# Four x buffers, a q transpose queued behind an x transpose, and a re-ordered first six microseconds

## The chip, the cores and the metric

One core of a Trainium2 chip. The metric is device time in microseconds (us) of one launch; the number compared is the median of several runs.

## What is computed

Linear attention with a feature map of exponentials, then a two-layer network with a squared ReLU. Cut to its core:

```python
# q, k, v: 8 batches x 8 heads x 576 tokens x 64; w_phi: 64 x 128
def phi(x):
    proj = einsum('bhsd,df->bhsf', x, w_phi)
    proj = proj - max(abs(proj), axis=-1, keepdims=True)
    return concatenate([exp(proj), exp(-proj)], axis=-1)
q_p, k_p = phi(q), phi(k)
kv = einsum('bhsf,bhsd->bhfd', k_p, v)
z = sum(k_p, axis=2)
x = einsum('bhsf,bhfd->bhsd', q_p, kv) / (einsum('bhsf,bhf->bhs', q_p, z)[..., None] + 1e-06)
# x becomes 4608 tokens x 512 (heads side by side); w_in: 512 x 2048, w_out: 2048 x 512
h = maximum(x @ w_in, 0)
out = (h * h) @ w_out
```

## The kernel before

**Work.** The eight batches run one after another through the attention, and 512 tokens of each batch form a chunk of the network; the last 64 tokens of all batches form a ninth chunk. The attention of batch b+1 is interleaved with the first layer of chunk b and the second layer of chunk b-1. TensorE does every product, ScalarE the exponentials, VectorE the maxima, the scaling and the squares; ReLU and copies out of PSUM are shared by the two. PSUM has eight banks, and every group of products is given a bank by a fixed list (`BASES`).

**Order.** The program is first laid down as a list of 1680 numbered operations (`Plan.add`); `ORDER` is a permutation of those numbers, and each engine executes its own operations in that order and never overtakes. An operation waits for its inputs, for its bank and for its buffer. `FILL` puts dummy products of a zero tile (`warm`, line 961) on TensorE ahead of the operations that it names, as (bank, count).

**The start.** Two pieces of k for batch 0 come by ScalarE's queue in float32 and are cast (operations 7 on VectorE, 8 on ScalarE); everything else of q, k, v and the weights comes by GpSimd's queue (13, 14, 12, 19, 9, 10, ... in this order). GpSimd also makes the identity matrix (operation 11, line 913) out of a tile that VectorE has zeroed (operation 5, line 238). With it TensorE transposes the first four blocks of k (40, line 320), VectorE copies them out (41), TensorE projects them (42, line 379), VectorE takes the maxima (48, line 386).

**From attention to the network.** For each block c of a batch (five blocks: four of 128 tokens, one of 64) the products with kv are made in two halves: NA (line 648, feature half one), a scaling of the bank by VectorE (SA, line 660), NB (line 648 again, added into the same bank), then a reciprocal (rd, line 670) and the division into `xo` (line 674), which also sets the bank free. NA of block c=1 and c=2 of batch 0 are operations 148 and 162, with 149/163 for SA and 150/164 for NB. In batch 0 TensorE transposes `xo`; in later batches a DMA transpose does (Xx, line 708, issued by SyncE, called SP here) and writes `xT`, which the first layer reads. `xo` is a ring of three buffers that all batches share, so block number n of the whole program uses buffer n mod 3.

**The first layer of chunk 0** starts block by block, as groups of 16 products of 128 columns (lines 813 and 799) for each quarter of `win`: 303/304 for quarter 0, 307/308 for quarter 1, 311/312 for quarter 2, 315/316 for quarter 3. Their ReLUs are 305, 309, 313, 317.

**SP's queue in the first half** holds, in this order: 373 (transpose of k of batch 2, writes `kT`), 374 (transpose of q of batch 2, writes `qT`), then 266, 275, 284, 293 (the four Xx of batch 1), 564 (transpose of k of batch 3), 302 (Xx of batch 1's short block), and stores. Operations of batch 1 that matter: 265, 274, 283, 292 write `xo` for the blocks c=0 to 3 (292 is block 8, and 266 reads block 5, the same buffer of three); 297 is NA of the short block, in the bank pair that 292 sets free. Operation 422 is the first product that reads batch 2's `qT` (line 347); 482 is the first product of chunk 1's first layer (line 788), and it needs all four Xx.

Of the kernel before, what the change touches and what calls it, by code (L numbers as in the profile page):

```python
# [7 lines left out]
F32 = mybir.dt.float32  # L8
# [100 lines left out]
def kernel(  # L109
# [61 lines left out]
    NQP = 3  # L171
    NQF = 2
# [3 lines left out]
    xo = ring("xo", 3, [8 * D])  # L176
    rden = ring("rden", 3, [8], F32)
# [130 lines left out]
    def attention(b):  # L308
# [279 lines left out]
        def out_halves():  # L588

            slot = qfeat[0]  # L590
            xs = xslot[0] % 3
# [42 lines left out]
        def out_ops(c):  # L634
# [30 lines left out]
            xs = xslot[0] % 3  # L665
# [407 lines left out]
}  # L1073
FILL = {
    40: (0, 26), 42: (0, 11), 74: (0, 5), 76: (0, 7), 58: (0, 10), 60: (4, 10), 92: (0, 7), 131: (0, 16),
    156: (7, 2), 101: (7, 2), 128: (7, 9), 134: (5, 4), 142: (5, 6),
}
TURNED = range(3, 8)
# [29 lines left out]
```

## Time and profile before

| | us |
|---|---|
| runs | 345.08, 345.47, 345.0 |
| median | 345.08 |
| span of the profiled execution, first to last instruction (the profile gives no other time for it) | 344.8 |
| TensorE busy in it | 335.5 |
| VectorE / ScalarE / GpSimd busy | 264.2 / 225.4 / 95.5 |

TensorE is busy for 97% of the span, so the way to read this profile is to look for the few places where TensorE does nothing and ask who ended each of them; time saved on another engine counts only if it ends one of those places sooner. TensorE's dummy products are counted as busy, too.

### The profile page before, as it was taken

Reading aid. Unit: us, or ns where it says so; the run is one execution under the profiler, and the core shown is the slowest. Engines: PE = TensorE matmul, PEld = TensorE weight load, DVE = VectorE, ACT = ScalarE, POOL = GpSimd, SP = SyncE. Lnnn points to the kernel's source line nnn. Section 1 sums busy time; section 2 is a strip of 40 time slices with the busy share of each in tenths; the row PEclk is TensorE's granted clock in tenths of the full one; section 3 lists DMA queues with packets and bytes.
Section 4 is the critical chain, followed back from the end, with each engine's and each line's share of the span. In section 5 each row is a group of like instructions: output and inputs, shape, how many; then the busy total and the mean of one; then the engine's idle time right before and its main releaser. Section 6 shows DMA issues by size and latency. Waiting matters only on the chain.

```text
span 344.8 us, 8417 instructions
## 1 busy us (share of the span) xinstructions
PE 335.5 (97%) x3389; PEld 188.3 (55%) x3389; DVE 264.2 (77%) x485; ACT 225.4 (65%) x393; POOL 95.5 (28%) x143
## 2 busy tenths in 40 slices
PE   8999999799999999999999999999999999999995
PEld 7679776444654555545545554565555444444443
DVE  4999999699877987788898999687876635757510
ACT  4999996489898898476887797798475503210031
POOL 8670671681730390104604051240000000000000
PEclk9999999999999999999999999999999999999999
DMA  9999999999999999999999999999864821101024
GB/s 139 179 206 202 199 132 157 153 118 205 170 175 172 227 165 185 195 182 183 171 207 172 199 164 195 188 154 168 196 125 96 157 62 38 63 0 61 32 68 115
DMA packets 142935, 51.51 MB, mean 149 GB/s; under 512 B 111472, under 2 KB 138416, under 8 KB 142896
## 3 DMA queue, kind: packets, MB, share of 16 engines
q1 hardware_dynamic: 97488, 32.35, 50.7%
q0 software_dynamic: 44960, 18.23, 46.7%
q8 instruction: 26, 0.43, 0.5%
q10 hardware_dynamic: 448, 0.39, 0.4%
q14 instruction: 13, 0.11, 0.1%
HBM read 36.73 MB, written 9.44 MB: 134 GB/s over the span
## 4 chain that ended last, share of the span: by engine, by line
PE 87%; DMA 6%; DVE 3%; ACT 1%; POOL 1%; issue 0%; POOLq 0%; DVEq 0%; SPq 0%
PE psum L788 32%; PE psum L882 31%; PE psum L648 5%; PE psum L462 5%; PE psum L347 5%; DMA xT<-xo 4%; DMA qpn<-qf 3%; PE psum L827 2%; PE psum L569 1%; DVE mk L405 1%; PE psum L813 1%; PE psum L799 1%; PE psum L846 1%; PE psum L450 1%; PE psum L320 1%; PE psum L961 1%
## 5 line engine op out<-in xcount | busy, mean ns | idle before, releaser
L882 PE MATMUL psum<-wout,h 128*128 128x512 bf16 x560 | 132.6, 380 | 0.0
L788 PE MATMUL psum<-xT,win 128*128 128x512 bf16 x448 | 106.1, 379 | 0.6 <-DMA xT<-xo 0.6
L765 ACT ACTIVATE hr<-psum 128x512 bf16<-128x512 f32 x98 | 57.1, 600 | 57.7 <-PE psum L788 50.2
L882 PEld LDWEIGHTS <-h 128*128 128x128 bf16 x560 | 51.1, 98 | 56.5 <-issue 0.3
L788 PEld LDWEIGHTS <-win 128*128 128x128 bf16 x512 | 46.7, 97 | 51.9 <-DMA xT<-xo 1.4
L774 DVE TENSOR_TENSOR h<-hr 128x512 bf16<-128x512 bf16 x144 | 56.0, 415 | 18.7 <-ACT hr L765 18.2
L544 ACT ACTIVATE qf<-psum 128x1024 bf16<-128x1024 f32 (+1 forms) x50 | 46.1, 939 | 5.5 <-PE psum L347 2.0
L405 DVE TENSOR_REDUCE mk<-psum 128x8 f32<-128x1024 f32 (+1 forms) x38 | 42.4, 1120 | 3.9 <-PE psum L347 2.0
L411 ACT ACTIVATE kn<-psum 128x1024 bf16<-128x1024 f32 (+1 forms) x38 | 35.7, 948 | 8.2 <-PE psum L347 4.7
L411 ACT ACTIVATE kp<-psum 128x1024 bf16<-128x1024 f32 (+1 forms) x38 | 35.8, 951 | 4.8 <-PE psum L347 4.0
L648 PEld LDWEIGHTS <-qpn 128*128 128x128 bf16 x624 | 27.5, 97 | 16.6 <-issue 3.1
L767 DVE TENSOR_SCALAR hr<-psum 128x512 bf16<-128x512 f32 x46 | 31.1, 684 | 5.7 <-PE psum L788 4.2
L660 DVE TENSOR_TENSOR psum<-psum,en 128x520 f32<-128x520 f32 (+1 forms) x39 | 27.2, 702 | 10.3 <-PE psum L648 6.1
L648 PE MATMUL psum<-kv,qpn 128*128 128x65 bf16 x624 | 30.6, 193 | 2.5 <-DVE xo L674 2.4
L269 POOL DMA_DIRECT2D xq<-in_q_dram x24 | 17.3, 727 | 55.2 <-DVE h L774 14.3
L531 DVE TENSOR_REDUCE mq<-psum 128x8 f32<-128x1024 f32 (+1 forms) x25 | 27.8, 1112 | 3.3 <-PE psum L347 2.5
L674 DVE TENSOR_TENSOR xo<-psum,rden 128x512 bf16<-128x512 f32 (+1 forms) x39 | 26.4, 684 | 3.7 <-DMA xT<-xo 3.2
L249 POOL DMA_DIRECT2D xk<-in_k_dram x27 | 20.0, 744 | 32.5 <-ACT en L508 16.0
L584 ACT ACTIVATE qpn<-psum 128x1024 bf16<-128x1024 f32 (+1 forms) x30 | 26.8, 955 | 2.5 <-PE psum L569 2.2
L195 ACT ACTIVATE ot<-psum 128x512 f32<-128x512 f32 x24 | 14.4, 598 | 20.3 <-PE psum L882 20.1
L428 DVE TENSOR_TENSOR va<-xv,va 128x1280 bf16<-128x1280 bf16 (+2 forms) x34 | 23.4, 714 | 0.8 <-ACT va L420 0.8
L249 POOL DMA_DIRECT2D xv<-in_v_dram x27 | 19.9, 744 | 14.7 <-PE psum L788 11.1
(79 smaller groups left out, 348.9 us busy)
## 6 DMA issues: line engine op xcount, KB each, us to landing
out_dram<-ot SPq DMA_DIRECT2D x32, 256.0 KB, 2.9
xk<-in_k_dram POOLq DMA_DIRECT2D x25, 128.0 KB, 5.6
xq<-in_q_dram POOLq DMA_DIRECT2D x24, 128.0 KB, 4.5
xv<-in_v_dram POOLq DMA_DIRECT2D x24, 128.0 KB, 5.0
win<-in_moe_w_in_dram POOLq DMA_DIRECT2D x4, 512.0 KB, 9.8
wout<-in_moe_w_out_dram POOLq DMA_DIRECT2D x4, 512.0 KB, 15.1
xq<-in_q_dram POOLq DMA_DIRECT2D x4, 256.0 KB, 6.4
out_dram<-ot SPq DMA_DIRECT2D x6, 128.0 KB, 2.3
```

Source lines behind the costliest of these rows:

```text
L249: pin(nc.gpsimd.dma_start(out=x[:, m0 + a * 512 : m0 + z * 512].rearrange("p (h x) -> p h x", x=4 * D), in_=src[b][2 * a : 2 * z, 0:512, : ...
L405: pin(nc.vector.tensor_reduce(out=mk_view(g), in_=ps2(pj)[:, :, : n * Fd].rearrange("p e (i f) -> p e i f", f=Fd), axis=AX.X, op=ALU.max, ...
L411: pin(nc.scalar.activation(out=dst[slot][:, :, :n, :].rearrange("p e i f -> p e (i f)"), in_=ps2(pj)[:, :, : n * Fd], func=ACT.Exp, scale= ...
L531: pin(nc.vector.tensor_reduce(out=mqb[:, c, :, :n], in_=ps2(pj)[:, :, : n * Fd].rearrange("p e (i f) -> p e i f", f=Fd), axis=AX.X, op=ALU ...
L544: pin(nc.scalar.activation(out=o, in_=i_, func=ACT.Exp, scale=sgn))
L648: pin(nc.tensor.matmul(out=o[:, u // 4, u % 4 * D1 : (u % 4 + 1) * D1], lhsT=qpn[slot][:, sg * half + u * m : sg * half + u * m + P], rhs= ...
L660: pin(nc.vector.tensor_tensor(out=o, in0=o, in1=enb[:m, c, :].rearrange("t (b h) -> t b h", b=2).to_broadcast([m, 2, 4, D1]), op=ALU.mult))
L765: pin(nc.scalar.activation(out=hr[sl], in_=ps1(g), func=ACT.Relu))
L767: pin(nc.vector.tensor_scalar(out=hr[sl], in0=ps1(g), scalar1=0.0, scalar2=None, op0=ALU.max))
L774: pin(nc.vector.tensor_tensor(out=dst, in0=i_, in1=i_, op=ALU.mult))
L788: pin(nc.tensor.matmul(out=o, lhsT=win[mc // 4][:, kc, mc % 4 * P : (mc % 4 + 1) * P], rhs=x, start=(kc == 0), stop=(kc == KC - 1)))
L882: pin(nc.tensor.matmul(out=ps1(g), lhsT=h2[c % 2][mc // 4][:, mc % 4, tt * P : (tt + 1) * P], rhs=wout[mc // 4][:, mc % 4, :], start=(mc = ...
```

## The change

Five edits. None changes what is computed.

1. `xo` and its reciprocals `rden` become rings of four (`NXO`).
2. In SP's queue 374 moves from ahead of 266 to right behind it; 275, 284, 293 follow as before.
3. On VectorE the zeroing of the identity's tile (5) moves ahead of the cast 7; on GpSimd the making of the identity (11) moves from the fourth place to the second, right behind the load 13 and so ahead of the loads 14 and 12.
4. The dummies: 27 for 26 ahead of operation 40, 6 for 11 ahead of 42, 6 for 7 ahead of 76 (a projection of k), 8 for 10 ahead of 58 (transposes of the piece of k that load 12 brings).
5. On TensorE the group 303/304 moves ahead of 311/312; before it came behind 162 (NA).

Nothing else moves on any engine: the remaining entries keep their order.

The diff, cut to the lines that differ in content (in the other lines of `ORDER` the numbers are only wrapped anew):

```diff
     NQP = 3
+    NXO = 4
     NQF = 2
...
-    xo = ring("xo", 3, [8 * D])
-    rden = ring("rden", 3, [8], F32)
+    xo = ring("xo", NXO, [8 * D])
+    rden = ring("rden", NXO, [8], F32)
...
-            xs = xslot[0] % 3
+            xs = xslot[0] % NXO
...
-    2, 0, 1, 13, 14, 12, 8, 6, 7, 5, 3, 4, 11, 19, 40, 41, 9, 42, 46, 48, 10, 74, 66, 47, 75, 15, 67, 76, 45, 43, 18,
+    2, 0, 1, 6, 5, 13, 11, 14, 12, 8, 7, 3, 4, 19, 40, 41, 9, 42, 46, 48, 10, 74, 66, 47, 75, 15, 67, 76, 45, 43,
...
-    191, 120, 142, 161, 138, 145, 143, 220, 146, 307, 308, 221, 147, 139, 311, 312, 309, 144, 233, 162, 313, 303,
-    140, 163, 304, 223, 148, 141, 164, 149, 322, 305, 222, 165, 310, 150, 166, 319, 323, 314, 151, 315, 306, 152,
+    119, 191, 120, 142, 161, 138, 145, 143, 220, 146, 307, 308, 221, 147, 139, 303, 304, 311, 312, 309, 144, 233,
+    162, 313, 140, 163, 223, 148, 141, 164, 149, 322, 305, 222, 165, 310, 150, 166, 319, 323, 314, 151, 315, 306,
...
-    240, 241, 248, 256, 228, 247, 259, 249, 229, 230, 260, 270, 231, 374, 285, 339, 343, 232, 250, 257, 271, 261,
-    344, 495, 262, 286, 354, 272, 263, 499, 287, 264, 265, 503, 273, 266, 274, 294, 345, 251, 295, 507, 252, 275,
+    244, 258, 240, 241, 248, 256, 228, 247, 259, 249, 229, 230, 260, 270, 231, 285, 339, 343, 232, 250, 257, 271,
+    261, 344, 495, 262, 286, 354, 272, 263, 499, 287, 264, 265, 503, 273, 266, 374, 274, 294, 345, 251, 295, 507,
...
-    40: (0, 26), 42: (0, 11), 74: (0, 5), 76: (0, 7), 58: (0, 10), 60: (4, 10), 92: (0, 7), 131: (0, 16),
+    40: (0, 27), 42: (0, 6), 74: (0, 5), 76: (0, 6), 58: (0, 8), 60: (4, 10), 92: (0, 7), 131: (0, 16), 156: (7, 2),
```

More of the change, by code (lines that the diff above doesn't have):

```diff
@@ L664, in out_ops @@
             add("PE", pe_cost(8, 0.0297), heads(1), r=[("qn", slot)] + kvs, w=[g], what="NB")
-            xs = xslot[0] % 3
+            xs = xslot[0] % NXO
             xslot[0] += 1
@@ L1074 @@
 FILL = {
-    40: (0, 26), 42: (0, 11), 74: (0, 5), 76: (0, 7), 58: (0, 10), 60: (4, 10), 92: (0, 7), 131: (0, 16),
-    156: (7, 2), 101: (7, 2), 128: (7, 9), 134: (5, 4), 142: (5, 6),
+    40: (0, 27), 42: (0, 6), 74: (0, 5), 76: (0, 6), 58: (0, 8), 60: (4, 10), 92: (0, 7), 131: (0, 16), 156: (7, 2),
+    101: (7, 2), 128: (7, 9), 134: (5, 4), 142: (5, 6),
 }
```

153 rows, old and new, of the table ORDER are left out of this document.

## The prediction

> **What bounds the kernel now.** I read the page first, then who waited for whom on TensorE and VectorE, then the instructions in order of time around each place where TensorE stood still.
>
> ```profile
> span 344.8 us, 8417 instructions
> PE 87%; DMA 6%; DVE 3%; ACT 1%; POOL 1%; issue 0%; POOLq 0%; DVEq 0%; SPq 0%
> ```
>
> TensorE carries 87% of the chain that ended last. So an edit pays only where TensorE idles, or in the first microseconds, where the chain runs over other engines. The waits, TensorE's two costliest after the start, and VectorE's on the x buffer (total, times, longest):
>
> ```profile
> PE psum L648 <- DVE xo L674: 2.4, 1, 2.4
> PE psum L788 <- DMA xT<-xo: 0.6, 1, 0.6
> DVE xo L674 <- DMA xT<-xo: 3.2, 1, 3.2
> ```
>
> One wait of 2.4 us stands out, and it looks like the tail of VectorE's 3.2. In order of time (start, duration, instruction; in brackets the idle time before it and who ended it):
>
> ```profile
> 49.81 5.17 SPq L331 DMA_TRANSPOSE kT<-xk  x1
> 55.23 3.87 SPq L331 DMA_TRANSPOSE qT<-xq  x1
> 55.28 0.69 DVE L674 TENSOR_TENSOR xo<-psum,rden 128x512 bf16<-128x512 f32 x1
> 59.15 7.51 SPq L708 DMA_TRANSPOSE xT<-xo  x4
> 61.23 1.90 PE L882 MATMUL psum<-wout,h 128*128 128x512 bf16 x8
> 61.38 0.20 DVE L670 RECIPROCAL rden<-psum 128x8 f32<-128x8 f32 x1
> 63.25 0.71 POOL L269 DMA_DIRECT2D xq<-in_q_dram  x1 [1.37 <-DMA qT<-xq]
> 64.75 0.69 DVE L674 TENSOR_TENSOR xo<-psum,rden 128x512 bf16<-128x512 f32 x1 [3.17 <-DMA xT<-xo]
> 65.50 0.40 PE L648 MATMUL psum<-kv,qpn 128*128 128x65 bf16 x8 [2.37 <-DVE xo L674]
> 67.80 0.40 PE L347 MATMUL psum<-wphi,qT 64*128 64x128 bf16 x8
> 71.59 1.90 PE L788 MATMUL psum<-xT,win 128*128 128x512 bf16 x8
> ```
>
> The reader is to see a loop. VectorE has its reciprocal at 61.58 but writes the fourth `xo` of batch 1 (292) only at 64.75. That buffer, the third of three, still has to be read by transpose 266, whose input was ready at 55.97 (55.28 + 0.69), but SP was inside the q transpose 374 until 59.10. TensorE's next NA (297) needs the banks that 292 sets free, so it stands from 63.13 to 65.50. How long such transposes take to land after issue (rows of the DMA issues, narrowed to these moments: the k transpose at 49.81, the q transpose at 55.23, the first and the last Xx):
>
> ```profile
> kT<-xk SPq DMA_TRANSPOSE x1, 9.4
> qT<-xq SPq DMA_TRANSPOSE x1, 7.5
> xT<-xo SPq DMA_TRANSPOSE x1, 5.5
> xT<-xo SPq DMA_TRANSPOSE x1, 2.7
> ```
>
> **Four buffers: -2.4 us.** With four, 292 (block 8) uses the buffer of block 4, which batch 0's TensorE transposes read long ago. It follows its reciprocal: 61.58 to about 62.3. TensorE arrives at 63.13, so 0.8 us of cover are left and the whole 2.37 goes. What is late next is the same order of work 2.4 us earlier; behind 65.5 TensorE's waits list only the 0.6 us of the second row above, an Xx that is issued behind TensorE's own products, so it moves with them and I leave it at 0.6 (bounds: gone, or twice that). The new buffer also shifts everything allocated behind it by 1 KB and 32 bytes; no row shows a price for that, and I take none.
>
> **q transpose behind the first Xx: 0, with thin cover.** By itself it frees 266 earlier, which four buffers no longer need. Its cost is on 374: 266 can go at 55.97, takes SP between 1.2 (the last of the four, from 292's end at 65.44 to 66.66) and 1.9 us (7.51 / 4), so 374 goes at 57.2 to 57.9 instead of 55.23. It had landed at 62.7 (55.23 + 7.5), 3.5 us behind the k transpose (49.81 + 9.4 = 59.2). In a queue that serves one after the other it now lands at 59.2 + 1.2 + 3.5 = 63.9; with its old latency at 65.4; with the k transpose's latency at 67.3. TensorE's first product on it (422) was at 67.80 and comes at about 65.8. I take 64 to 65.4, in which case the move is hidden by 0.4 to 1.8 us; the cost at the far end is 1.5 us. Queued behind 374 on SP are 275, 284 and 293: the last landed at 65.5 + 2.7 = 68.2, behind the same six transfers as now, and the first layer that reads it came at 71.59, now 69.6. GpSimd's load at 63.25, which waits for 374 to land, goes 1.2 to 2.7 us later and its queue with it; this is an input of a batch two further on, and TensorE does not wait for a load behind 26 us in this trace, so nothing is charged.
>
> **The first microseconds: -0.4 us.**
>
> ```profile
> 0.99 2.95 PE L961 MATMUL psum<-warm 128*128 128x128 bf16 x26 [0.99 <-DVE warm L235]
> 2.99 0.73 POOL L249 DMA_DIRECT2D xk<-in_k_dram  x1
> 3.60 0.42 ACT L195 ACTIVATE xk<-ot 128x256 bf16<-128x256 f32 x1 [0.67 <-DMA ot<-in_k_dram]
> 4.16 0.59 PE L320 MATMUL psum<-ident,xk 128*128 128x128 bf16 x4 [0.21 <-POOL ident L913]
> 4.53 1.22 PE L961 MATMUL psum<-warm 128*128 128x128 bf16 x11
> 4.78 0.42 DVE L193 COPY kT<-psum 128x512 bf16<-128x512 bf16 x1 [0.59 <-PE psum L320]
> 5.68 0.40 PE L379 MATMUL psum<-wphi,kT 64*128 64x128 bf16 x8
> 6.15 0.69 DVE mk L386
> 8.46 0.39 PE L320 MATMUL psum<-ident,xk 128*128 128x128 bf16 x4
> xk<-in_k_dram POOLq DMA_DIRECT2D x1, 128.0 KB, 5.0
> 17.47 1.48 POOL L292 DMA_DIRECT2D win<-in_moe_w_in_dram  x2 [1.92 <-DMA xk<-in_k_dram]
> 17.77 0.38 PE L320 MATMUL psum<-ident,xk 128*128 128x128 bf16 x4
> ```
>
> The identity is now made before the load that stood at 2.99, so it is there before 3.7 and the 0.21 wait goes. Instead the 27 dummies end at 0.99 + 27 x 0.113 = 4.04 and ScalarE's cast at 4.02: the transposes start at about 4.07, 0.09 earlier. VectorE's copy then ends at 5.11. The projection 42 could start 0.06 behind it (the hand-over seen from 65.44 to 65.50), and 6 dummies at 0.111 (1.22 / 11) end by then: 5.17 against 5.68, which is 0.5 earlier. At 0.11 per dummy TensorE still ran at half of its later pace (0.056, from the 16 products below) and the projection may partly do so now, which I price at 0.1. VectorE is the chain from 6.15 on, so -0.4 reaches the steady part. Bounds: -0.5, or 0 if a load becomes the limit. The load at 2.99 lands at 8.0, its reader stood at 8.46, behind dummies of which two go; moved back by the identity's making, at most 0.4 (from 3.72, where that load's issue ended, to 4.16, where the identity had released TensorE), it would still land at 8.4. Batch 1's k let GpSimd go on at 17.47 and is read at 17.77: 0.3 of cover for a shift of 0.4. The other dummies cut (76, 58) lie under VectorE's work there and count nothing.
>
> **Two groups swapped: +0.8 us.**
>
> ```profile
> 27.85 1.06 PE L813 MATMUL psum<-xT,win 128*128 128x128 bf16 x16
> 28.75 0.41 PE L648 MATMUL psum<-kv,qpn 128*128 128x65 bf16 x8
> 28.95 0.60 ACT L765 ACTIVATE hr<-psum 128x512 bf16<-128x512 f32 x1
> 29.89 0.65 PE L648 MATMUL psum<-kv,qpn 128*128 128x65 bf16 x16
> 30.37 1.05 PE L799 MATMUL psum<-xT,win 128*128 128x128 bf16 x16
> 30.39 0.71 DVE L660 TENSOR_TENSOR psum<-psum,en 128x520 f32<-128x520 f32 x1 [0.18 <-issue]
> ```
>
> Before: 311 at 27.85, NA 162 at 28.75, then the group 303 as cover while ScalarE empties 311's bank (313, 28.95 to 29.55) and VectorE scales 162's; at 29.89 NA 148, which needs that bank, and NB 164, which needs that scaling. Now 303 stands ahead, and 311, 162, 148, 164 follow each other without cover. In the old clock: 311 at 28.75, NA 162 at 29.65. ScalarE's 313 starts 0.2 behind 311's stream, at 29.85, and ends at 30.45, so NA 148 starts at 30.5 and not at 29.9. VectorE starts a scaling 0.5 behind its NA (29.89 to 30.39), so at 30.15, and ends at 30.86: NB 164 at 30.9. It takes 0.24 (half of 29.89 to 30.37), and the next group starts at 31.15 instead of 30.37. TensorE has no idle time from there to 63 us, so nothing absorbs it. Bounds: +0.5 if the two engines are quicker off the mark, +1.0 if ScalarE, which has its next operations 0.9 later, delays one more bank.
>
> **Sum.** -0.4 + 0.8 - 2.4 = -2.0 on the profiled span: 344.8 to 342.8. The runs' median lies 0.28 above that span, so 343.1.
>
> **The rivals.** *Everything gained and a little more:* the swap costs 0.5 and the 0.6 us wait goes too: 342.2. For it: that wait hangs on a queue that gets emptier. Against: its Xx is fed by the engines. 12%.
>
> *The q transpose becomes the new wait.* It lands with the k transpose's latency, 67.3 instead of 65.8: 1.5 is given back, 344.6, and less if it is in between. For it: 9.4 was seen right ahead of it in the same queue. Against: part of the 7.5 it had was spent behind the k transpose. 12%, two thirds of it below the bound of "same".
>
> *Slower:* the same place with a longer wait. Past 67.8 TensorE is later than before; by more than 0.2% (0.7 us, about what a measurement of this kernel can tell from no change) if 374 lands behind 68.5, some 11 us after its issue. At 12 us, 69.5, the kernel ends at 346.8. For it: 266 is now ahead of it, and GpSimd's loads (63.25 and on) run beside it. Against: no transpose row above exceeds 9.4. 7%.
>
> *The dummies were needed.*
>
> ```profile
> 6.00:7.00 1.00, 1.00 (x22) 0.99 (x19) 0.85 (x2) 0.89 (x2) 1.00 (x3) 1.00 1.66 186
> 7.00:8.00 1.00, 1.00 (x24) 0.69 (x22) 1.00 (x3) 1.00 (x3) 1.00 (x2) 1.00 1.71 182
> ```
>
> These stretches (second and third number: TensorE's busy time and instructions) hold 46 products. If TensorE stayed at the early pace through them, each would take up to 0.055 longer: 2.5 us at most, about half of it hidden by VectorE: 344.4. The granted clock, second from last but one, reads 1.00 throughout, so only the spacing of products speaks of a slow phase. The Trainium skill, "TensorE: Matmul & The Clock Gate", Part 1, speaks against cutting dummies: it says that the array starts at half rate and is released after a sustained busy window that is not aligned to the kernel's start; the spacing of 0.113 and later 0.056 agrees. Against the rival: TensorE stays busy from 0.99 to 5.1 without a gap over 0.1, less idle than before. 6%.
>
> *It doesn't do what it says:* 292 waits for something other than its buffer, and the 2.4 stays: 345.2 + 0.3 = 345.5. Against: the inferred releaser fits the three-buffer count and the time exactly. 5%.
>
> **How the numbers follow.** The forecast has 58% and its own range 342.6 to 343.7. The range 342.2 to 344.6 adds the better case and the late q transpose up to its price, and leaves out the last part of the others. Faster by over 0.2% (below 344.4): 58 + 12 + 8 + 4 = 82%. Same: 4 + 2 + 5 = 11%. Slower: 7%.
>
> **What would show it.** Right: no wait of TensorE on the `xo` write near 63 us; 292 within 0.2 us of its reciprocal; at about 30 us a wait of NA 148 on ScalarE's ReLU and of NB on the scaling, some 0.7 together; the first maxima near 5.7. Wrong: TensorE waiting for the q transpose at 65, or for any DMA between 65 and 140 longer than 1 us; a start no earlier than 6.1; no wait at 30.

## The result, and the profile after

The kernel after takes 346.66 us in the median (345.69 to 353.59, 22 runs), the kernel before, run beside it, 344.94 us. The ratio is 1.0053, 95% interval [1.0038, 1.0069]: the change makes the kernel 0.5% slower, where 0.6% faster was forecast. One disturbed execution of this kernel (353.59), and further on one of no_swap (350.12) and one of qmove_only (349.97), are left out of the ratios.

The page of after, its span and the engines of the chain that ended last:

```profile
span 345.5 us, 8373 instructions
PE 76%; DMA 10%; ACT 5%; DVE 5%; issue 2%; SPq 0%; ACTq 0%
```

TensorE carried 87% of the chain before; here it carries 76%, and transfers have gone from 6% to 10%. Such shares differ between executions of one kernel, too (after_a, the same kernel profiled again, has 91% and 3%), so they say little alone. The waits of this execution name the places (total, times, longest):

```profile
PE psum L789 <- DMA xT<-xo: 1.6, 1, 1.6
PE psum L348 <- DMA kT<-xk: 1.0, 1, 1.0
PE psum L649 <- ACT hr L766: 0.4, 1, 0.4
POOL xq L270 <- DMA qT<-xq: 3.0, 1, 3.0
```

VectorE's and TensorE's waits around `xo` are gone. A wait for an x transpose has grown from 0.6 to 1.6 us, one for a k transpose is new, NA 148 waits 0.4 us for ScalarE, and GpSimd waits 3.0 us for the moved q transpose, where it waited 1.37. In order of time, on after's line numbers (one higher than before's in these functions):

```profile
4.04 0.42 ACT L196 ACTIVATE xk<-ot 128x256 bf16<-128x256 f32 x1 [1.11 <-DMA ot<-in_k_dram]
6.15 0.69 DVE L387 TENSOR_REDUCE mk<-psum 128x4 f32<-128x512 f32 x1 [0.79 <-PE psum L380]
...
26.77 1.07 PE L814 MATMUL psum<-xT,win 128*128 128x128 bf16 x16
29.69 0.41 PE L649 MATMUL psum<-kv,qpn 128*128 128x65 bf16 x8
30.54 0.81 PE L649 MATMUL psum<-kv,qpn 128*128 128x65 bf16 x16 [0.44 <-ACT hr L766]
31.18 1.06 PE L800 MATMUL psum<-xT,win 128*128 128x128 bf16 x16
...
56.81 1.20 SPq L709 DMA_TRANSPOSE xT<-xo  x1
58.25 3.31 SPq L332 DMA_TRANSPOSE qT<-xq  x1
62.20 0.20 DVE L671 RECIPROCAL rden<-psum 128x8 f32<-128x8 f32 x1
62.43 0.69 DVE L675 TENSOR_TENSOR xo<-psum,rden 128x512 bf16<-128x512 f32 x1
65.70 0.71 POOL L270 DMA_DIRECT2D xq<-in_q_dram  x1 [3.00 <-DMA qT<-xq]
66.08 0.40 PE L348 MATMUL psum<-wphi,qT 64*128 64x128 bf16 x8
...
97.99 4.80 SPq L332 DMA_TRANSPOSE kT<-xk  x1
102.80 0.69 DVE L675 TENSOR_TENSOR xo<-psum,rden 128x512 bf16<-128x512 f32 x1
102.90 2.92 SPq L549 DMA_TRANSPOSE qpn<-qf  x1
105.92 2.87 SPq L709 DMA_TRANSPOSE xT<-xo  x2
110.03 2.33 PE L789 MATMUL psum<-xT,win 128*128 128x512 bf16 x10 [1.61 <-DMA xT<-xo]
...
189.10 0.28 PE L348 MATMUL psum<-wphi,kT 64*128 64x128 bf16 x4 [1.00 <-DMA kT<-xk]
```

At 66.08 us TensorE reaches batch 2's first q product, which stood at 67.80 before: 1.72 us ahead, as forecast (-0.4 + 0.8 - 2.4 = -2.0, less the start, whose maxima stand at 6.15 as before). So against this one profile of before the forecast holds up to 66 us. Two things remained to be found out: who takes the lead back at 110 and 189 us, and whether the lead was there at all in an ordinary execution of before.

### The profile page after: what moved, and what is told of

The parts are those of the page before. It is cut to its first block, busy times and chain, and to the rows that moved or that the text cites. A ratio compares the mean times of both kernels' runs of the same rounds, so it can differ in the third digit from the quotient of the medians.

```text
span 345.5 us, 8373 instructions
## 1 busy us (share of the span) xinstructions
PE 333.9 (97%) x3352; PEld 188.1 (54%) x3382; DVE 264.6 (77%) x485; ACT 225.4 (65%) x393; POOL 95.6 (28%) x143
## 4 chain that ended last, share of the span: by engine, by line
PE 76%; DMA 10%; ACT 5%; DVE 5%; issue 2%; SPq 0%; ACTq 0%
PE psum L883 28%; PE psum L789 26%; DMA qpn<-qf 7%; PE psum L649 5%; PE psum L348 4%; PE psum L463 4%; DMA kT<-xk 2%; PE psum L828 2%; DVE mk L406 1%; ACT qf L545 1%; ACT kp L412 1%; ACT kn L412 1%; PE psum L570 1%; PE psum L814 1%; DVE mq L532 1%
## 5 line engine op out<-in xcount | busy, mean ns | idle before, releaser
L883 PE MATMUL psum<-wout,h 128*128 128x512 bf16 x530 | 128.5, 379 | 2.0 <-issue 0.6
```

Source lines behind the costliest of these rows:

```text
L883: pin(nc.tensor.matmul(out=ps1(g), lhsT=h2[c % 2][mc // 4][:, mc % 4, tt * P : (tt + 1) * P], rhs=wout[mc // 4][:, mc % 4, :], start=(mc = ...
```

## The experiments

All comparisons are with the kernel before, run on the same chip beside them (medians 344.77, 344.74, 344.64 and 344.17 us in the four groups). The edits combine few pieces: B four buffers, Q the q transpose moved, S the swapped groups, I the early identity, D the other dummies. The kernel after is B+Q+S+I+D.

**Buffers alone, and each of Q and S taken out.** Base of the first and last is the kernel before, of the other two the kernel after.

buffers4 (B):
```diff
+    NXO = 4
-    xo = ring("xo", 3, [8 * D])
+    xo = ring("xo", NXO, [8 * D])
```


> The kernel before with four x buffers and nothing else. Theory Q (the moved q transpose holds GpSimd's queue and makes the DMAs late): here it stays ahead, so the 2.4 us wait near 65 us goes and most of the gain stays, about 1.5 to 2.4 us faster than before (0.9930 to 0.9957 of it). Theory S (the swapped groups put everything 0.8 us late): also 1.5 to 2.4 faster. Theory F (the transposes and loads between 59 and 110 us fill the DMA, whatever is gained ahead of them is handed back there): the wait near 65 goes, a wait for an xT transpose near 110 grows from 0.6 to about 2 to 3 us, and the time is within 0.6 us of before.

no_swap (after without S; on `ORDER`):
```diff
-    303, 304, 311, 312, 309, 144, 233, 162, 313, 140, 163, 223,
+    311, 312, 309, 144, 233, 162, 313, 303, 140, 163, 304, 223,
```


> The changed kernel with the group 303/304 back behind NA 162. Theory S: the 0.8 us goes and the loads of batch 3, which wait for engine steps, start 0.8 us earlier with it, so the later waits shrink too: 1.2 to 1.8 us faster than the changed kernel, about the time of before. Theory Q: only the 0.8 us that TensorE stood still: 0.6 to 0.9 faster than changed. Theory F: TensorE arrives 0.8 earlier near 110 and waits that much longer: within 0.4 us of changed.

no_qmove (after without Q):
```diff
-    260, 270, 231, 285,
+    260, 270, 231, 374, 285,
...
-    273, 266, 374, 274,
+    273, 266, 274,
```


> The changed kernel with the q transpose 374 back ahead of 266. Theory Q: GpSimd waits about 1.4 us for it near 63 us and not 3.0, batch 3's k transpose goes 0.5 to 0.8 earlier, the waits near 110 and 189 shrink: 1.0 to 1.8 us faster than changed. Theory S and theory F: within 0.5 us of changed.

swap_only (S): the lines of no_swap in reverse, on the kernel before.

> The kernel before with the group 303/304 moved ahead of 311/312 and nothing else. All theories: TensorE stands 0.7 to 0.8 us near 30 us. Theory S: the loads and transposes go with it, total 0.8 us or more slower than before. Theory F and theory Q: the wait near 65 us, which a DMA ended, takes most of it up, since that DMA is not issued later: 0 to 0.4 us slower.

Measured: buffers4 1.0004 [0.9976, 1.0032]; no_swap 1.0071 [1.0041, 1.0101]; no_qmove 1.0030 [1.0007, 1.0054]; swap_only 1.0032 [1.0015, 1.0049]. The largest term of the forecast, alone, shows no gain; the interval leaves room for one of 0.8 us, not for the 2.4 forecast nor for the 1.5 to 2.4 that two of the theories expected. And the swap alone costs, yet taking it out of the kernel after did not help there, which two of the theories had expected; no_swap's runs spread from 344.74 to 348.95 us.

**Is the 2.4 us wait always there?** before_a and before_b are the kernel before itself, with no edit, profiled again. qmove_only is Q on the kernel before. ramp_only is I+D on it:

```diff
-    2, 0, 1, 13, 14, 12, 8, 6, 7, 5, 3, 4, 11, 19, 40,
+    2, 0, 1, 6, 5, 13, 11, 14, 12, 8, 7, 3, 4, 19, 40,
...
-    40: (0, 26), 42: (0, 11), 74: (0, 5), 76: (0, 7), 58: (0, 10),
+    40: (0, 27), 42: (0, 6), 74: (0, 5), 76: (0, 6), 58: (0, 8),
```

> The kernel before, profiled a second time. Theory V (the 2.4 us wait near 65 us is not fixed: it hangs on how long the k transpose of batch 2 takes to land, which differs from execution to execution): the wait comes out anywhere from 0 to 2.4 us, and with a latency of the k transpose below about 7 us it is under 0.5. Rival C (constant): the wait is again 2.2 to 2.6 us.

> The kernel before, profiled a third time. As for the second: theory V: the wait near 65 us follows the latency of batch 2's k transpose and differs from the other profiles by over 0.5 us in at least one of them; rival C: 2.2 to 2.6 us in each.

> The kernel before with the q transpose 374 behind the first Xx 266 and nothing else (three x buffers). All: no wait of TensorE for xo near 65 us, since 266 lands near 61. Theory Q (the move makes batch 2's q and with it GpSimd's queue and batch 3's transposes late): landing of batch 2's q at 64 to 65.5, of batch 3's k above 84, the wait near 110 us grows to over 1 us, total 0.5 to 1.5 us slower than before. Theory F (only the total of transfers counts): within 0.5 us of before. The prediction's own term: 2 us faster.

> The kernel before with the early identity and the other dummies, nothing else. The prediction's term: first maxima near 5.7 us, 0.4 us faster. Rival L (the second piece of k on ScalarE's queue and then batch 1's k set the start): TensorE waits 0.3 to 0.7 us more for k by DMA in the first 20 us, steady part at the same time as before, within 0.4 us of before in total.

The kernel before in before_b, first from its page:

```profile
span 343.0 us, 8387 instructions
```

then the DMA issues near 50 us (median us from issue to landing):

```profile
kT<-xk SPq DMA_TRANSPOSE x1, 6.5
qT<-xq SPq DMA_TRANSPOSE x1, 6.5
```

and in order of time:

```profile
50.14 4.35 SPq L331 DMA_TRANSPOSE kT<-xk  x1
54.73 2.67 SPq L331 DMA_TRANSPOSE qT<-xq  x1
57.46 6.14 SPq L708 DMA_TRANSPOSE xT<-xo  x4
61.20 1.41 POOL L269 DMA_DIRECT2D xq<-in_q_dram  x2
61.42 0.20 DVE L670 RECIPROCAL rden<-psum 128x8 f32<-128x8 f32 x1
61.69 0.69 DVE L674 TENSOR_TENSOR xo<-psum,rden 128x512 bf16<-128x512 f32 x1
...
102.03 0.69 DVE L674 TENSOR_TENSOR xo<-psum,rden 128x512 bf16<-128x512 f32 x1
102.32 3.22 SPq L708 DMA_TRANSPOSE xT<-xo  x2
108.77 2.56 PE L788 MATMUL psum<-xT,win 128*128 128x512 bf16 x11 [1.12 <-DMA xT<-xo]
```

The same program, the same three buffers, and no wait: 292 is written at 61.69, 0.07 us behind its reciprocal. The k transpose that took 9.4 us to land took 6.5, SP came through the q transpose 1.7 us sooner (57.40 instead of 59.10), and the third buffer had been read in time. before_a has no such wait either, and a span of 343.0, though its k transpose was not quick (in order of time, then among the DMA issues):

```profile
48.89 4.06 SPq L331 DMA_TRANSPOSE kT<-xk  x1
kT<-xk SPq DMA_TRANSPOSE x1, 8.8
```

It was issued 1.25 us sooner than in before_b, and so landed at 57.7. The wait came again in ramp_only, which has three buffers too; its k transpose among the DMA issues, and the wait in order of time:

```profile
kT<-xk SPq DMA_TRANSPOSE x1, 10.2
```

```profile
62.38 0.20 DVE L670 RECIPROCAL rden<-psum 128x8 f32<-128x8 f32 x1
65.26 0.69 DVE L674 TENSOR_TENSOR xo<-psum,rden 128x512 bf16<-128x512 f32 x1 [2.68 <-DMA xT<-xo]
66.00 0.40 PE L648 MATMUL psum<-kv,qpn 128*128 128x65 bf16 x8 [1.89 <-DVE xo L674]
```

So the wait follows the moment at which the k transpose lands, and not the time it takes alone: 56.6 and 57.7 us in before_b and before_a without the wait, 59.2 and 60.6 (50.41 + 10.2) in the first profile and ramp_only with it. SP left the q transpose behind it at 57.40, 57.59, 59.10 and 60.27. The Trainium skill, "DMA: Bandwidth & Descriptors", section "Queues, rings and completion order", says that each DMA engine takes turns between the queues it has work for; that would let GpSimd's loads stretch a transpose of SP's, and a spread from 6.5 to 10.2 us fits, but no run here takes those loads away.

Times: before_a 344.75 and before_b 344.76 us (one run each), qmove_only 1.0016 [0.9995, 1.0038], ramp_only 1.0030 [1.0003, 1.0058]. The last came out slower than expected (1.0 us, where at most 0.4 was expected), though its interval reaches down to that.

**The two halves of the start, and the kernel after without Q and S.** ident_only takes only the `ORDER` line above, fill_only only the `FILL` line, on the kernel before. buf_ramp is B+I+D. after_a is the kernel after, with no edit.

> The kernel before, with the making of the identity moved ahead of the second load on GpSimd's queue, and the old dummies. The ramp's two halves together measured 1.0030 [1.0003, 1.0058]; there the first maxima came at 5.47 us instead of 6.15, and then TensorE waited 0.5 to 0.7 us for the next k. Theory G (the loads behind the identity are what costs): this half alone gives the price, 1.002 to 1.004, about 346.0, and the k and q loads of the first 10 us land 0.4 us or more later than in the three profiles of before. Theory D (the dummies cut cost it): no difference here, 0.999 to 1.001. Theory N (the ramp's result was noise of that run): no difference here nor with the dummies alone.

> The kernel before, with only the numbers of dummy products changed (27, 6, 6 and 8 instead of 26, 11, 7 and 10). Theory G: 0.999 to 1.000; fewer dummies ahead of the projection bring the first maxima 0.4 us forward, and the next k load, where it is late, takes that back. Theory D: 1.002 to 1.004, with the products between 6 and 13 us at wider spacing. Theory N: 0.999 to 1.001.

> The kernel after without its swap and without the move of the q transpose: four buffers, early identity and new dummies. Theory S+Q (each of the two costs its own 0.2 to 0.3%, whatever else is there): 1.000 to 1.002, at least 0.3% below the kernel after on the same chip. Theory R (the ramp carries the loss): 1.003 or more, within 0.2% of the kernel after.

> The kernel after itself, profiled and timed again beside the three others. All theories: 1.004 to 1.007. Theory F (the gain of the start and of the buffers is handed back to late loads and transposes): a wait of TensorE on a DMA somewhere behind 60 us again, of 0.5 us or more, but not at the same two places as in the first profile (110 and 189 us), since which landing is late varies from execution to execution. If it stands at the same places with the same length, it is the order's and not chance.

Measured: ident_only 0.9997 [0.9982, 1.0013], fill_only 0.9986 [0.9969, 1.0004], buf_ramp 0.9971 [0.9946, 0.9997], after_a 1.0037 [1.0017, 1.0056]. Neither half of the start has a price of its own (N, not G or D); ramp_only's 1.0030 was not borne out. Without Q and S the loss is gone. In after_a TensorE's wait for the x transpose stands at 110.05 us again, 1.2 us long, while the one at 189 is not there: that one belonged to the execution. A wait near 110 is not peculiar to the new order either (before_b has 1.12 us, ident_only 1.19); what is peculiar to it comes out below, where the profiles are compared.

**Q and S apart, and Q doubled.** buf_ramp_b is B+I+D again, no_swap_b adds Q, no_qmove_b adds S (the lines shown above). q_later puts the q transpose one x transpose further back than Q does:

```diff
-    260, 270, 231, 374, 285,
+    260, 270, 231, 285,
...
-    252, 275, 296,
+    252, 275, 374, 296,
```

> The kernel after without its swap and without the move of the q transpose, a second time, as the base of the three beside it. It measured 0.9971 [0.9946, 0.9997]: 0.996 to 0.999 expected. If the gain was chance, 1.000. GpSimd's load that waits for batch 2's q transpose waits 0.5 to 1.4 us near 62, and TensorE waits for no k transpose.

> The base with the q transpose moved. Theory Q (the move carries most of the loss, by way of GpSimd's queue: its load waits some 3 us for that transpose near 65, so batch 3's k and q arrive late, and TensorE waits 0.5 to 1.5 us at its products or some 1 us more at a later Xx): 0.3 to 0.5% above the base. Theory P (only the swap costs, the move nothing): equal to the base.

> The base with the two groups swapped. Theories Q and P alike: 0.77 us more at 25 to 34 us of the span, as in four profiles so far, so 0.2% above the base, and nothing given back later. If it is at 0.4% or more, the swap costs also behind 34 us.

> The base with the q transpose moved further, behind the second of batch 1's x transposes instead of the first. Theory Q: at least what the move itself costs, 0.4 to 1.0% above the base; GpSimd's load waits 4 us or more near 66, and TensorE waits for the q transpose itself at 65 or for batch 3's k transpose. Theory P: within 0.2% of the base, unless TensorE waits for the q transpose itself.

| | pieces | median us | ratio to before |
|---|---|---|---|
| buf_ramp_b | B+I+D | 344.54 | 0.9998 [0.9972, 1.0024] |
| no_qmove_b | B+I+D+S | 345.20 | 1.0014 [0.9987, 1.0042] |
| no_swap_b | B+I+D+Q | 345.54 | 1.0033 [1.0002, 1.0063] |
| q_later | B+I+D, Q twice as far | 347.43 | 1.0080 [1.0053, 1.0107] |

The medians put S at 0.66 us and Q at 1.00 us, and Q twice as far at 2.89 us. The intervals against the kernel before are as wide as the single steps (and no_swap, the same kernel as no_swap_b, had 1.0071 in its group), so it is better to compare these kernels with each other, as they ran on one chip. Of the 144 pairs of a run of no_swap_b and a run of buf_ramp_b, no_swap_b is the slower in 124, and the means lie 1.18 us apart; every run of q_later is slower than every run of buf_ramp_b. So moving the q transpose back costs time, and more the further back it goes. For S alone the same count is less clear (the means lie 0.73 us apart). The waits of no_swap_b, then of q_later, then q_later's waiting product in order of time:

```profile
POOL xq L270 <- DMA qT<-xq: 2.8, 1, 2.8
PE psum L789 <- DMA xT<-xo: 1.3, 1, 1.3
```

```profile
POOL xq L270 <- DMA qT<-xq: 5.5, 1, 5.5
PE psum L348 <- DMA qT<-xq: 1.5, 1, 1.5
PE psum L789 <- DMA xT<-xo: 1.3, 1, 1.3
```

```profile
67.10 0.40 PE L348 MATMUL psum<-wphi,qT 64*128 64x128 bf16 x8 [1.54 <-DMA qT<-xq]
```

In q_later most of the 1.9 us beyond no_swap_b is TensorE's own 1.54 us wait for the q transpose; in no_swap_b TensorE does not wait for it at all, and GpSimd does. So q_later shows that the move costs, but it can't show that a longer wait of GpSimd's costs more.

**All profiles side by side.** VectorE's instructions are complete in every trace, so the start of the same instruction can be compared. The columns give how many us each kernel loses (+) or gains (-) against before_b: up to 15.5 us, between 24.9 and 34.3, between 56.2 and 70.4, and from there to 328.5 (all on before_b's clock). The last two are GpSimd's wait for batch 2's q transpose, and when batch 3's k transpose landed.

| | pieces | start | 25-34 | 56-70 | behind 70 | GpSimd's wait | k landed |
|---|---|---|---|---|---|---|---|
| before (first profile) | | -0.04 | 0.0 | +2.53 | -0.64 | 1.4 | 82.74 |
| before_a | | +0.48 | 0.0 | 0.0 | -0.48 | 0 | 79.97 |
| before_b | | 0 | 0 | 0 | 0 | 0 | 80.45 |
| swap_only | S | +0.13 | +0.77 | 0.0 | -0.52 | 0 | 81.18 |
| ramp_only | I+D | +0.96 | 0.0 | +2.05 | -1.04 | 1.6 | 82.88 |
| ident_only | I | +0.21 | 0.0 | 0.0 | -0.35 | 0 | 79.44 |
| fill_only | D | +0.51 | 0.0 | 0.0 | -0.25 | 0 | 81.01 |
| buffers4 | B | -0.12 | 0.0 | 0.0 | -0.10 | 0 | 81.40 |
| buf_ramp | B+I+D | -0.22 | 0.0 | 0.0 | -1.74 | 0.5 | 80.30 |
| buf_ramp_b | B+I+D | +0.43 | 0.0 | 0.0 | -0.97 | 0 | 78.98 |
| no_qmove | B+I+D+S | +0.12 | +0.77 | +0.35 | +0.10 | 0 | 81.68 |
| no_qmove_b | B+I+D+S | +1.10 | +0.77 | 0.0 | -0.06 | 0 | 82.02 |
| qmove_only | Q | -0.08 | 0.0 | 0.0 | +0.74 | 3.6 | 85.02 |
| no_swap | B+I+D+Q | +0.19 | 0.0 | 0.0 | +1.29 | 3.2 | 85.90 |
| no_swap_b | B+I+D+Q | +0.42 | 0.0 | 0.0 | -0.08 | 2.8 | 83.74 |
| after | all | +0.01 | +0.77 | 0.0 | +1.79 | 3.0 | 84.77 |
| after_a | all | +0.44 | +0.77 | 0.0 | -0.33 | 3.0 | 84.73 |
| q_later | B+I+D, Q twice | +0.18 | 0.0 | +1.61 | +1.29 | 5.5 | 86.87 |

Read by columns: S costs 0.77 us wherever it is, and nothing where it is not. The `xo` wait delays the kernel in two of the seven profiles with three buffers and the q transpose in its old place (in swap_only and ident_only VectorE waits 0.5 to 0.6 us for it and TensorE not at all), and in none with four buffers or with Q; the +0.35 of no_qmove is a wait for an x transpose by the first layer. With Q (the five kernels from qmove_only to after_a) GpSimd waits 2.8 to 3.6 us and batch 3's k lands at 83.7 to 85.9; without it, 0 to 1.6 and 79.0 to 82.9. The two sets do not overlap. Behind 70 us the five with Q lose 0.68 us on the mean and the twelve without gain 0.50: 1.2 us between them, with a spread of some 0.5 to 0.9 from one execution to another. One stretch divides the two sets cleanly: between 104 and 120 us of before_b's clock the six profiles with a moved q transpose (q_later is the sixth) lose 0.3 to 0.9 us against before_b, and of the twelve others none loses over 0.1. Part of it is given back later.

The path from GpSimd to TensorE in after: batch 3's inputs are issued behind the held load, and its k transpose lands at 84.77 instead of 80.45 (before_b). GpSimd issues the next loads at 83.36, 0.79 us later than before_b (82.57), which is little more than the swap's 0.77; but they land later still, the last of batch 4's k at 97.86 instead of 95.56, and SP waits for it ahead of the k transpose at 97.99, which stood at 96.20 in before_b (SP's wait between 80 and 115 us; total, times, longest):

```profile
SPq L332 <- DMA xk<-in_k_dram: 1.0, 1, 1.0
```

SP has this wait, 0.5 to 1.0 us, in five of the six profiles with a moved q transpose (not in qmove_only), and among the twelve others only in no_qmove, 0.2 us. Behind it the x transpose that the first layer needs goes at 105.92, though its input was ready at 103.49 (102.80 + 0.69). In buf_ramp, which shows no wait of TensorE there, the same transpose goes at 101.52:

```profile
101.52 3.36 SPq L709 DMA_TRANSPOSE xT<-xo  x2
107.27 4.05 PE L789 MATMUL psum<-xT,win 128*128 128x512 bf16 x18
```

In no_swap the wait comes earlier instead: TensorE waits 1.1 us for batch 3's k transpose itself at 85.94 us, and then 1.0 us for the x transpose at 110.17.

**A version that beats both?** buf_ramp, the kernel after without Q and S, is faster than the kernel after. Against the kernel before it measured 0.9971 and then 0.9998; that it beats the kernel before is not established.

## Why the prediction was wrong, point by point

- **Four buffers, -2.4: the mechanism was right, the size was not.** 292 follows its reciprocal (62.40 to 62.43) and the wait is gone. But the term was read from one execution in which it happened. Over the seven profiles it is (2.53 + 2.05) / 7 = 0.65 us on the mean, and in five of the seven 0; buffers4's interval fits both. This is the step that failed most.
- **"The runs' median lies 0.28 above that span."** before_a's run of 344.75 us has a span of 343.0, after's run of 347.31 one of 345.5: the time is some 1.8 above the span of the same execution (1.7 to 1.9 in every run). The first profile's 344.8 therefore belonged to an execution of an estimated 346.6 us, 1.5 above the median of 345.08; 4 of before's 22 runs took 346.4 or more. The forecast subtracted a saving from a longer execution than usual and then compared the rest with the ordinary ones. With an ordinary span of 343.0 and without the wait, its own other terms (-0.4 + 0.8) would have given 345.2. That is 2.1 of the 3.6 us by which the forecast missed; the rest is mainly the q transpose and the start.
- **q transpose moved, 0.** The forecast of its landing (64 to 65.4) held (58.25 + 6.9 = 65.2): GpSimd's load goes at 65.70 and TensorE's product at 66.08 without waiting. The rivals that priced a wait of TensorE for it were wrong. What failed is "TensorE does not wait for a load behind 26 us in this trace, so nothing is charged": the held load delays the batch behind it, and TensorE then waits for that batch's transpose, or for the x transpose that stands behind it on SP. Measured: 1.0 us by the medians of no_swap_b and buf_ramp_b, 1.2 by their means and by the traces.
- **The 0.6 us wait "moves with them".** It did not. The x transpose is fed by TensorE's products but held by SP's queue, where it stands behind a k transpose and a feature transpose. Its wait ranged from none to 1.6 us in these profiles. The text had named the sign of this failure: a wait on a DMA between 65 and 140 us longer than 1 us.
- **The start, -0.4.** The first maxima do come earlier: at 5.65 us on the mean of the ten profiles with I and D, at 5.94 in the six with neither. But each start ranges widely (5.20 in buf_ramp to 6.15 in after; 5.56 in swap_only to 6.52 in before_a). In after they stand at 6.15, since ScalarE's input landed late and its cast stood at 4.04 instead of the 3.60 counted on. And an early start can find the next k not there: ramp_only, with its maxima at 5.47, waits 1.7 us in two places for it. At 15.5 us the ten profiles with I and D together stand 0.36 behind before_b on the mean, the six with neither 0.06: nothing gained. The bound "0 if a load becomes the limit" was the right one.
- **The swap, +0.8.** Right: 0.77 in all five profiles that have it, where it was forecast. From NA 162 to the next products behind it takes 0.85 us instead of 0.24 (29.69 to 30.54; before, 28.75 to 28.99), for which the profile lists a wait of 0.44 on ScalarE's ReLU; from there to the next group, over the scaling, 0.64 instead of 0.48 (to 31.18; before, 29.89 to 30.37). From the group at 26.77 to the one at 31.18 it takes 4.41 us, beside 3.64 before (26.73 to 30.37).
- **The dummies were needed.** No price was found: fill_only 0.9986 [0.9969, 1.0004].

Put together by the means of the traces: +0.3 (start) + 0.77 (swap) + 1.2 (q transpose) - 0.65 (buffers) = +1.6 us, beside 346.66 - 344.94 = 1.72 measured. These are means over few executions that differ by half a microsecond and more, so agreement to 0.1 us is partly luck. That the move of the q transpose costs some 1 us is shown by no_swap_b beside buf_ramp_b. That it goes by GpSimd's held loads is read from the traces; no run took that wait alone away, so another path beside it is left open.

## What to carry to other kernels

A wait of a microsecond behind a DMA in a single profile may be that execution's own: profile the unchanged kernel two or three times, and compare its time with the span of the same execution, before a term of the sum is built on it. When a transfer is moved back, look past its first reader: whoever waits for it on a queue that feeds a later batch passes the delay on, and here it came back to the busiest engine 20 to 45 us later. Small edits with a fixed price on the busiest engine (0.77 us here, to two digits in every execution) weigh more than larger ones whose gain depends on how late a transfer happens to be.

## What the runs showed of the hardware

- The same DMA transpose took 6.5, 8.8 and 9.4 us from issue to landing in three executions of one unchanged kernel (before_b, before_a, before), and such differences, with those of the issue, decided which wait a profile showed.
- Lateness early in the kernel is partly absorbed: before_a was 0.48 us behind before_b from 15 to 97 us and level with it from 113 us on, since at 108.77 before_b had to wait 1.12 us for a transpose that before_a, which started at 108.75, found landed.
